# A recorded attention and two-network kernel: the list scheduler takes other transfer rates, and the weight sums of the second network leave from one contiguous corner

## The chip, the cores and the metric

The kernel runs on one core of a Trainium2 chip. The metric is the device time of one execution in microseconds (us), the median of several runs. TensorE (PE) multiplies matrices, VectorE (DVE), ScalarE (ACT) and GpSimd (POOL) work on elements, and SyncE (SP) issues the DMA transfers, which 16 DMA engines of the core carry out. SBUF is the on-chip memory with 128 partitions; PSUM holds the eight banks that matmuls write.

## The reference

Windowed attention with 32 global tokens, then two feed-forward networks over all 2304 tokens, all in float32.

```python
# q_l, k_l, v_l: (4, 8, 512, 64); q_g, k_g, v_g: (4, 8, 32, 64)
s_g = scale * q_g @ [k_g, k_l].T
out_g = softmax(s_g) @ [v_g, v_l]
s_ll = where(abs(pos_q - pos_k) <= 32, scale * q_l @ k_l.T, -1e9)
s_l = concatenate([scale * q_l @ k_g.T, s_ll])
out_l = softmax(s_l) @ [v_g, v_l]
x = concatenate([out_g, out_l]) as (2304, 512)
# first network: 512 -> 1536 -> 512
g = x @ w_gate
x = (g * sigmoid(g) * (x @ w_val)) @ w_out
# second network: 512 -> 2048 -> 512
h = x @ w_in
out = (maximum(h, 0) + alpha * minimum(h, 0)) @ w_out2
```

The weights of both networks come to the chip as float64 words.

## The kernel before, in words

**The work.** Every product is made in three passes over operands that are split into a high and a low part (type fp32r), so that float32 accuracy is kept. The first network is done in visits: `visit1(b, fs, ...)` takes the 512 tokens of batch b through one half of the hidden columns, f by f: `mm12` makes the gate bank `g` and the value bank `v` from the inputs `xa` (12 matmuls each), ACT makes `sg` (silu), DVE the product `t`, ACT the high half of `h` and DVE its low half, and `down(f)` adds 12 matmuls into the four banks `acc0` to `acc3`. A third visit (line 1239 on) and the whole second network use seven products of half-size blocks in place of eight, for which sums of weight blocks are wanted beside the weights.

**Preparing weights.** A piece of float64 weights is loaded into a buffer `dbl` (`dbl_tile`, two buffers, dbl_111 and dbl_112), turned into float32 in a buffer `raw` (raw_131, raw_132) by `convert_steps` (L753): two ACT instructions (raw<-dbl, then dbl<-dbl in place) and three on DVE. For the second network the generator `w2_prepare` (L861) does that for 16 pieces. `out_to` (L868) splits each piece into its high and low half in the `dbl` buffer and stores it to DRAM (`w2s`; the names in the profile are w2sx and w2so, 1 MB each). For each of the eight pieces of the input weights it also makes the sums of blocks (`block_sums`, L850) in a second raw buffer. Those sums (key "s", w2ss in the profile) leave another way while the recording is on: the high half is written by ACT into a free part of `xa`, namely the last 128 of the 640 columns in each of its eight rows, and stored from there, 8 pieces of 512 bytes for each partition; the low half is made in place and stored from raw. `pumper` (L1079) calls the generator: at each pump a counter grows by `P["w2n"]`, and the generator goes one step for each whole number reached. What is left of the generator when the recording ends goes on in the straight part. The sums of the first network's weights (`w1_sums`, L823) are made by DVE in the two buffers of `ex` (y_139 and y_166 or y_167 in the listings) and stored as w1ss4v, w1ss5g and so on; the split weights of the first network are stored as w1s and loaded again later (w<-w1s4g).

**The order.** The first part of the kernel (attention, and the first network for batches 0 to 2, about 421 us) isn't issued as it is written. `Planner` (L58) records each instruction with its reads and writes; `price` (L124) gives it a duration, `graph` (L154) finds what depends on what, and `order` (L180) simulates the four engines and picks, at each step, the ready instruction with the earliest due time. Transfers are simulated as one channel that moves `DMA` KB a microsecond; `flush` (L265) then issues everything in that order on each engine. All these instructions have line L272 in the profile. The buffers were given out when the work was recorded, so the order decides when each comes free. What follows `flush` (the third visit, the second network) is written straight. The lines of `order` on a transfer:

```python
if e == "sync":
    y += 0.45
    dma = max(dma, y + 1.0) + atoms[i][0].lat
    done[i] = [dma + 0.9]
```

Of the kernel before, what the change touches and what calls it, by code (L numbers as in the profile page):

```python
# [10 lines left out]
F32 = mybir.dt.float32  # L11
F32R = mybir.dt.float32r
# [4 lines left out]
ACTF = mybir.ActivationFunctionType  # L17
ALU = mybir.AluOpType

B, H, S, G, D = 4, 8, 512, 32, 64  # L20
# [4 lines left out]
N3 = 320  # L25
NAMES = ("b11", "t2", "t3", "t1", "b21", "t4", "b22")
NT = 384
# [10 lines left out]
    lo0=0.0, lo1=0.0, lo2=0.0, lo3=0.0, hi0=0.0, hi1=0.25, hi2=0.25, hi3=0.5,  # L38
    wl0=2, wl1=2, wd=2, tsim=False,
    hq0=0.0, hq1=0.0, hq2=0.0, hq3=0.0, pr_s=0, pr_pv=0, pr_conv=0, pr_hilo=0, pr_st=0, pr_ld=0, pr_h=0,  # L40
    pr_xp=0, pr_acc=0, pr_lda=0, wage=3, w2n=1.7, w2max=200, cp0=0.5, cp1=0.0,
)


# [13 lines left out]
class Planner:  # L58
# [6 lines left out]


    ENGINES = ("tensor", "vector", "scalar", "sync")
    TABLE, DMA, START, LAST = 1.28, 405.0, 0.75, 10.0

    def __init__(self, tc):  # L70
        self.tc, self.nc = tc, tc.nc
# [108 lines left out]
    def order(self):  # L180
        atoms, preds = self.atoms, self.graph()
        N = len(atoms)
        size = [sum(o.cost for o in a) for a in atoms]
        eng = [a[0].eng for a in atoms]
        before = [sorted({j for e in p.values() for j, _ in e}) for p in preds]
        for i, b in enumerate(before):
            assert not b or b[-1] < i
        after = [[] for _ in atoms]
        for i, b in enumerate(before):
            for j in b:  # L190
                after[j].append(i)
        at, target = 0.0, [0.0] * N
        for i in range(N):
            target[i] = at
            if eng[i] == "tensor":
                at += size[i]
        due = [0.0] * N
        for i in reversed(range(N)):
            d = target[i] if eng[i] == "tensor" else min(target[i] + self.SLACK, at - self.LAST)
            for j in after[i]:  # L200
                d = min(d, due[j] - size[i] - atoms[i][-1].lat)
            due[i] = d
        free = {e: self.START for e in self.ENGINES}
        table, dma = None, 0.0
        left = [len(b) for b in before]
        done = [None] * N
        ready = {e: {} for e in self.ENGINES}

        def data(i):
            t, off = 0.0, 0.0  # L210
            for m, o in enumerate(atoms[i]):
                for j, k in preds[i].get(m, ()):
                    x = done[j][k] - off
                    if eng[j] == eng[i]:
                        x -= atoms[j][k].lat if eng[i] != "sync" else 0.0
                    elif eng[i] == "tensor":
                        x += self.MARGIN
                    t = max(t, x)
                off += o.cost
            return t  # L220

        for i in range(N):
            if not left[i]:
                ready[eng[i]][i] = 0.0
        plan = []
        while len(plan) < N:
            best = None
            for e in self.ENGINES:
                if ready[e]:
                    t = max(free[e], min(ready[e].values()))  # L230
                    if best is None or t < best[0]:
                        best = (t, e)
            t, e = best
            cand = [i for i, r in ready[e].items() if r <= t + self.LOOK]

            def rank(i):
                f = atoms[i][0].table
                return due[i] + (self.SWITCH if f and f != table else 0.0)

            i = min(cand, key=rank)  # L240
            x = max(t, ready[e].pop(i))
            f = atoms[i][0].table
            if f and f != table:
                x += self.TABLE
                table = f
            done[i] = []
            y = x
            if e == "sync":
                y += 0.45
                dma = max(dma, y + 1.0) + atoms[i][0].lat  # L250
                done[i] = [dma + 0.9]
            else:
                for o in atoms[i]:
                    y += o.cost
                    done[i].append(y + o.lat)
            free[e] = y
            plan.append(i)
            for j in after[i]:
                left[j] -= 1
                if not left[j]:  # L260
                    ready[eng[j]][j] = data(j)
        self.end = max(free.values())
        return plan
# [22 lines left out]
class Slots:  # L286
# [11 lines left out]
    def next(self, tag):  # L298
        return self.turn.get(tag, 0) % self.sizes[tag][0]
# [22 lines left out]
def kernel(  # L322
# [11 lines left out]
    nc = Planner(tc)  # L334
# [14 lines left out]
    const = ctx.enter_context(tc.tile_pool(name="const", bufs=1))  # L349
# [17 lines left out]

    ident = const.tile([128, 128], F32, name="ident")
    ex = Slots(const, {"y30": (1, 1024), "y31": (1, 1024)})
    xa = const.tile([128, 2, 4, 640], F32R, name="xa")  # L370
    yp = [const.tile([128, 2, 4, 256], F32, name=f"yp{b}") for b in range(B - 1)]
    y3 = {}

# [308 lines left out]
    def dbl_tile():  # L682
        i = ring["d"] = (ring["d"] + 1) % ND
        if i == 2 and st["k"] < mark[2] - 4:
            return yp[2].rearrange("p h m c -> p (h m c)").bitcast(I64)
        return dblp.tile([128, 1024], I64, tag="dbl", name="dbl")
# [154 lines left out]
    w2s = {}  # L841
# [19 lines left out]
    def w2_prepare():  # L861

        def land(n):
            dbl = dbl_tile()
            nc.sync.dma_start(out=dbl, in_=w2[n // 2, n % 2])
            return dbl

        def out_to(key, raw):  # L868
            w2s[key] = dram.tile([128, 2, 1024], F32, name="w2s%s%d" % key)
            if key[0] != "s" or not nc.recording:  # L870
                t = dbl.bitcast(F32R).rearrange("p (h c) -> p h c", h=2)
                yield from split(t, raw)
                nc.sync.dma_start(out=w2s[key], in_=t.bitcast(F32))
                return
            hi, lo = xa.rearrange("p h k c -> p (h k) c")[:, :, S:640], raw.rearrange("p (k c) -> p k c", c=128)
            st["tail"] = True
            nc.scalar.activation(out=hi, in_=lo, func=ACTF.Copy)
            yield
            nc.vector.tensor_tensor(out=lo.bitcast(F32R), in0=lo, in1=hi, op=ALU.subtract)
            nc.sync.dma_start(out=w2s[key][:, 0].rearrange("p (k c) -> p k c", c=128), in_=hi.bitcast(F32))  # L880
            nc.sync.dma_start(out=w2s[key][:, 1], in_=raw)
            st["tail"] = False

        dbl = land(0)
        for n in range(2 * NJ):
            ahead = land(n + 1) if n + 1 < 2 * NJ else None
            yield
            raw = raw_tile()
            yield from convert_steps(dbl, raw)
            yield  # L890
            if n % 2 == 0:
                s = raw_tile()
                yield from block_sums(s, raw)
            yield from out_to(("xo"[n % 2], n // 2), raw)
            if n % 2 == 0:
                for _ in range(1 if nc.recording else 6):
                    yield
                yield from out_to(("s", n // 2), s)
            dbl = ahead
# [136 lines left out]
    if True:  # L1036
# [92 lines left out]
        p = pumper(P["ns1"], mark[2] + LAG, P["wr0"], P["g1"])  # L1129
        visit1(0, GA, False, p, after_f=reload(GB, GA))  # L1130
        visit1(0, GB, True, p, boundary=lambda: xprep(1))
        p = pumper(P["ns2"], mark[3] + LAG, P["wr2"], P["g2"])
        visit1(1, GB, False, p, after_f=summing(reload(GA, GB)))
        visit1(1, GA, True, p, after_f=summing(lambda f, ps: None), boundary=lambda: xprep(2))
        p = pumper(P["ns3"], mark[4] + 9, P["wr3"], P["g3"])
        visit1(2, GA, False, p, after_f=reload(GB, GA))

        ops1, w3, place, sums = {}, {}, {}, {}
# [20 lines left out]
        def oper(flat, n):  # L1159
            return flat[:, 0:4 * n].rearrange("p (h k c) -> p h k c", h=2, k=2)  # L1160
# [21 lines left out]
        def third():  # L1182

            while wq:
                wload(True)
            while st.get("tail"):
                next(w2gen)
            flat = xa.rearrange("p h k c -> p (h k c)")
            for i, name in enumerate(("t3", "t1", "b21", "t4")):
                ops1[name] = oper(flat[:, 4 * N3 * i:4 * N3 * i + 4 * N3], N3)  # L1190
            x_split(2, ops1["b11"], (0, 0))
            for name in ("t2", "t3", "t1"):
                x_split(2, ops1[name], sums[name])
            x_split(2, ops1["b21"], (1, 0))
            x_split(2, ops1["t4"], sums["t4"])

        visit1(2, GB, True, p, after_f=before_third, boundary=third)
        while wq:
            wload(True)
# [19 lines left out]
        ops = {}  # L1219
# [109 lines left out]
        for j in range(NF1 // 2):  # L1329
# [10 lines left out]
            h = hring[j % 2]  # L1340
# [37 lines left out]
        x_split(0, ops["t1"], t1)  # L1378
        t4 = next(sums)[1]
        x_split(0, ops["t3"], next(sums)[1])  # L1380
        flat = xa.rearrange("p h k c -> p (h k c)")
        for i, name in enumerate(("b21", "t4", "b22")):
            ops[name] = oper(flat[:, 4 * NT * i:4 * NT * i + 4 * NT], NT)
        x_split(0, ops["b21"], (1, 0))
        x_split(0, ops["t4"], t4)
        x_split(0, ops["b22"], (1, 1))
# [194 lines left out]
```

## Time and profile before

| | before |
|---|---|
| median of 3 runs | 897.06 us (897.03 to 897.11) |
| the profiled execution | 896.01 us |
| its span in the profile | 894.2 us |
| TensorE busy | 866.7 us (97%) |
| DVE busy | 692.1 us (77%) |
| ACT busy | 528.2 us (59%) |
| DMA queue 1 | 238.19 MB, 70.8% of the 16 engines' span |

The span is what the profiler saw of the instructions; the profiled execution's own time is 1.8 us longer. A row of an engine's timeline gives the start in us, the busy time, the engine, the line, the operation with the tile that it writes and the one that it reads, the size, how many follow one another, and in brackets the idle time before it with what ended that. On SP a row is the issue of a transfer; when it landed is in the view of DMA issues. A row of stretches gives the stretch, its length, the busy time of PE, PEld (weight loads), DVE, ACT and POOL with their instructions, the granted clock as a share of full speed, the share of time that the DMA engines were busy, and GB/s.

### The profile page before, as it was taken

How to read it: one execution, taken by the hardware profiler on the slowest of the kernel's cores; microseconds unless marked ns; L12 is line 12 of the kernel's file. 1: busy time of each engine (PE TensorE's matmuls, PEld its weight loads, DVE VectorE, ACT ScalarE, POOL GpSimd, SP SyncE). 2: the span in 40 equal slices, each digit the busy share in tenths (PEclk: the TensorE clock that was granted, in tenths of full speed). 3: DMA queues.
4: the chain of work that ended last, by engine and by line, in shares of the span. 5: the costliest groups of instructions: out<-in, count | busy, mean ns of one | idle time of the engine just before them, and what ended most of it. 6: DMA issues, size and time to landing. Idle time of an engine off the chain costs nothing.

```text
span 894.2 us, 17315 instructions
## 1 busy us (share of the span) xinstructions
PE 866.7 (97%) x6868; PEld 749.0 (84%) x6868; DVE 692.1 (77%) x1442; ACT 528.2 (59%) x1051; POOL 0.7 (0%) x6
## 2 busy tenths in 40 slices
PE   6799999999899999899999999999999999999997
PEld 5577778787688787778999999999999999989996
DVE  4997889969778865688666677777896777977776
ACT  5889999767667688554333346434555434554442
POOL 0000000000000000000000000000000000000000
PEclk9999999999999999999999999999999999999999
DMA  9899899798986789985656665546375554675731
GB/s 360 300 393 414 334 354 361 289 351 321 407 358 219 301 323 370 335 306 192 212 189 206 237 247 212 228 156 267 142 266 229 211 213 172 252 272 225 280 141 60
DMA packets 48833, 239.30 MB, mean 268 GB/s; under 512 B 4848, under 2 KB 13680, under 8 KB 26480
## 3 DMA queue, kind: packets, MB, share of 16 engines
q1 hardware_dynamic: 48752, 238.19, 70.8%
q8 instruction: 54, 0.88, 0.4%
q14 instruction: 27, 0.22, 0.1%
HBM read 183.38 MB, written 54.79 MB: 266 GB/s over the span
## 4 chain that ended last, share of the span: by engine, by line
PE 78%; DMA 10%; ACT 5%; DVE 5%; issue 1%; SPq 0%; ACTq 0%; DVEq 0%
PE ps_acc L1451 21%; PE ps_g L1239 9%; PE ps_v L1239 9%; PE ps_a L1239 8%; PE acc L272 8%; PE v L272 7%; PE g L272 7%; PE a L272 5%; PE ps_acc L1296 3%; DMA dbl<-in_w_dram 3%; DMA w2so<-dbl 2%; PE ps_a L1296 2%; DMA w2sx<-dbl 2%; DVE dbl L272 1%; DMA yp<-in_w_dram 1%
## 5 line engine op out<-in xcount | busy, mean ns | idle before, releaser
L1451 PE MATMUL ps_acc<-w,hring 128*128 128x512 f32 x816 | 194.2, 391 | 0.0
L1451 PEld LDWEIGHTS ps_acc<-w,hring 128*128 128x128 f32 x816 | 152.0, 188 | 30.1 <-ACT hring L1420 0.3
L272 PE MATMUL acc<-h,w 128*128 128x512 f32 x432 | 108.2, 399 | 3.1 <-ACT h L272 2.2
L272 PE MATMUL g<-xa,w 128*128 128x512 f32 x432 | 107.8, 398 | 2.5 <-ACT sg L272 1.6
L272 PE MATMUL v<-xa,w 128*128 128x512 f32 x432 | 107.1, 396 | 0.2 <-issue 0.2
L1415 ACT ACTIVATE r<-c 128x384 f32<-128x384 f32 (+1 forms) x96 | 47.8, 498 | 92.9 <-DVE c L1247 92.9
L272 PEld LDWEIGHTS acc<-h,w 128*128 128x128 f32 x432 | 81.0, 191 | 22.3 <-ACT h L272 2.5
L1456 DVE TENSOR_TENSOR oacc<-ps_acc,oacc 128x512 f32<-128x512 f32 x119 | 81.9, 691 | 22.2 <-PE ps_acc L1451 20.9
L272 PEld LDWEIGHTS g<-xa,w 128*128 128x128 f32 x432 | 78.9, 188 | 22.8 <-ACT sg L272 3.0
L272 PEld LDWEIGHTS v<-xa,w 128*128 128x128 f32 x432 | 79.3, 188 | 18.6 <-issue 1.8
L1420 ACT ACTIVATE hring<-g 128x384 fp32r<-128x384 f32 (+1 forms) x96 | 48.6, 506 | 55.9 <-DVE g L1417 55.6
L272 ACT ACTIVATE e<-e,mx 128x128 f32<-128x128 f32 (+1 forms) x136 | 57.2, 423 | 14.6 <-DVE mx L272 14.2
L1421 DVE TENSOR_TENSOR hring<-g,hring 128x384 fp32r<-128x384 f32 (+1 forms) x96 | 51.1, 532 | 18.9 <-ACT hring L1420 16.1
L1417 DVE SCALAR_TENSOR_TENSOR g<-g,nal,r 128x384 f32<-128x384 f32 (+1 forms) x96 | 56.8, 591 | 10.4 <-ACT g L1416 9.7
L272 ACT ACT_TABLE_LOAD x46 | 59.0, 1283 | 8.0 <-PE g L272 6.6
L1416 ACT ACTIVATE g<-c 128x384 f32<-128x384 f32 (+1 forms) x96 | 47.9, 499 | 13.9 <-DVE hring L1421 13.9
L1239 PE MATMUL ps_g<-xa,w 128*128 128x320 f32 (+1 forms) x288 | 53.3, 318 | 0.2
L1239 PE MATMUL ps_v<-xa,w 128*128 128x320 f32 (+1 forms) x288 | 53.2, 319 | 0.1
L1239 PE MATMUL ps_a<-w 128*128 128x384 f32 (+1 forms) x288 | 51.4, 326 | 0.0
L1239 PEld LDWEIGHTS ps_g<-xa,w 128*128 128x128 f32 x288 | 47.1, 188 | 1.9 <-ACT p L1255 0.4
L1239 PEld LDWEIGHTS ps_v<-xa,w 128*128 128x128 f32 x288 | 46.8, 188 | 1.6 <-DVE u L1263 0.4
L1239 PEld LDWEIGHTS ps_a<-w 128*128 128x128 f32 x288 | 47.9, 188 | 0.1
(211 smaller groups left out, 1397.7 us busy)
## 6 DMA issues: line engine op xcount, KB each, us to landing
dbl<-in_w_dram SPq DMA_DIRECT2D x28, 1024.0 KB, 8.0
w<-w2so SPq DMA_DIRECT2D x24, 1024.0 KB, 5.3
w<-w2sx SPq DMA_DIRECT2D x24, 1024.0 KB, 4.8
w<-w2ss SPq DMA_DIRECT2D x24, 1024.0 KB, 6.4
v<-in_v_dram SPq DMA_DIRECT2D x15, 1024.0 KB, 10.0
qk<-in_qk_dram SPq DMA_DIRECT2D x14, 688.0 KB, 9.5
w2sx<-dbl SPq DMA_DIRECT2D x8, 1024.0 KB, 8.0
w2so<-dbl SPq DMA_DIRECT2D x8, 1024.0 KB, 9.7
```

The lines of the kernel that those rows point to most:

```text
L272: last[o.eng] = getattr(getattr(self.nc, o.eng), o.op)(*o.args, **o.kw)
L1239: nc.tensor.matmul(out=o[:, 0:n], lhsT=left(name, a, k), rhs=x[name][:, b, k, 0:n], start=(i == 0), stop=(i == 5),)
L1296: mm = nc.tensor.matmul(out=o, lhsT=a, rhs=x, start=(first and e == 0 and not second), stop=((j, f, e) == (NF1 // 2 - 1, 0, 2) and i not i ...
L1415: nc.scalar.activation(out=rr, in_=u, func=ACTF.Relu)
L1416: nc.scalar.activation(out=g, in_=u, func=ACTF.Relu, scale=-1.0)
L1417: nc.vector.scalar_tensor_tensor(out=g, in0=g, scalar=nal[:, i:i + 1], in1=rr, op0=ALU.mult, op1=ALU.add)
L1420: nc.scalar.activation(out=hi, in_=g, func=ACTF.Copy)
L1421: nc.vector.tensor_tensor(out=lo, in0=g, in1=hi, op=ALU.subtract)
L1451: nc.tensor.matmul(out=o, lhsT=a, rhs=x, start=(i == 0), stop=(i == 5))
L1456: nc.vector.tensor_tensor(out=oacc[tb], in0=o, in1=oacc[tb], op=ALU.add)
```

## The change

It has three parts. In `order`, the channel of the simulation moves 385 KB/us, not 405; a transfer may start 0.3 us after its issue begins, not 1.45, and is seen by others 1.9 us after its end, not 0.9. `w2n` is 2, not 1.7. And `xa` is allotted as one flat tile: its first 4096 columns are the eight rows of 512 columns, and the 1024 columns behind them are `tail`, into which the high half of the sums is written, and from which it is stored, 4 KB in one piece for each partition.

```diff
-    ... w2n=1.7, ...
+    ... w2n=2, ...
...
-    TABLE, DMA, START, LAST = 1.28, 405.0, 0.75, 10.0
+    TABLE, DMA, START, LAST = 1.28, 385.0, 0.75, 10.0
...
             if e == "sync":
+                dma = max(dma, y + 0.3) + atoms[i][0].lat
+                done[i] = [dma + 1.9]
                 y += 0.45
-                dma = max(dma, y + 1.0) + atoms[i][0].lat
-                done[i] = [dma + 0.9]
...
-    xa = const.tile([128, 2, 4, 640], F32R, name="xa")
+    xall = const.tile([128, 16 * N3], F32R, name="xa")
+    xa = xall[:, 0:8 * S].rearrange("p (h k c) -> p h k c", h=2, k=4)
+    tail = xall[:, 8 * S:8 * S + 1024]
...
-            hi, lo = xa.rearrange("p h k c -> p (h k) c")[:, :, S:640], raw.rearrange("p (k c) -> p k c", c=128)
             st["tail"] = True
-            nc.scalar.activation(out=hi, in_=lo, func=ACTF.Copy)
+            nc.scalar.activation(out=tail, in_=raw, func=ACTF.Copy)
             yield
-            nc.vector.tensor_tensor(out=lo.bitcast(F32R), in0=lo, in1=hi, op=ALU.subtract)
-            nc.sync.dma_start(out=w2s[key][:, 0].rearrange("p (k c) -> p k c", c=128), in_=hi.bitcast(F32))
+            nc.vector.tensor_tensor(out=raw.bitcast(F32R), in0=raw, in1=tail, op=ALU.subtract)
+            nc.sync.dma_start(out=w2s[key][:, 0], in_=tail.bitcast(F32))
             nc.sync.dma_start(out=w2s[key][:, 1], in_=raw)
```

In the two places where all of `xa` is used as one flat area (`third` and the end of the third visit), `xall` takes the place of the rearranged tile.

What these numbers do to the order is seen in the listings of the instructions of each engine, here at three places. The first is SP where the first network's sums w1ss4v are stored. Before:

```order
L272 DMA w2sx_165<-dbl_111 128x2048
L272 DMA w2ss_167<-raw_132 128x1024
L272 DMA w_134<-w1s1g 128x2048
L272 DMA dbl_111<-in_w_dram 128x1024
L272 DMA w1ss4v<-y_166 128x1024
L272 DMA w2so_170<-dbl_112 128x2048
L272 DMA w1ss4g<-y_139 128x1024
L272 DMA w_135<-w1s2g 128x2048
```

With the change, where that store stands now:

```order
L272 DMA dbl_112<-in_w_dram 128x2x512
L272 DMA w1s8o<-w_144 128x2048
L272 DMA w1s10g<-w_137 128x2048
L272 DMA w1ss4v<-y_167 128x1024
L272 DMA v_110<-in_v_dram 128x2048
L272 DMA v_108<-in_v_dram 128x2048
L272 DMA w1s11g<-w_138 128x2048
L272 DMA dbl_112<-in_w_dram 128x1024
```

The store has gone from SP's row 76 to its row 62, ahead of the loads of the next attention pairs' v.

The second place is ACT in the second visit to batch 1, behind the pt (the transposed probabilities) of an attention pair; dbl_111 holds a piece of the second network's weights there. Before:

```order
L272 ACTIVATE h_151<-t_150 128x512
L272 ACTIVATE dbl_112<-raw_132 128x1024
L272 ACTIVATE raw_131<-dbl_111 128x1024
L272 ACTIVATE dbl_111<-dbl_111 128x1024
L272 ACT_TABLE_LOAD
L272 ACTIVATE sg_148<-g_103 128x512
L272 ACTIVATE yp_95<-a_114 128x2x256
L272 ACTIVATE dbl_111<-raw_131 128x1024
L272 ACTIVATE h_152<-t_150 128x512
```

With the change:

```order
L272 ACTIVATE h_151<-t_150 128x512
L272 ACTIVATE dbl_112<-raw_132 128x1024
L272 ACT_TABLE_LOAD
L272 ACTIVATE sg_148<-g_103 128x512
L272 ACTIVATE yp_95<-a_114 128x2x256
L272 ACTIVATE raw_131<-dbl_111 128x1024
L272 ACTIVATE dbl_111<-dbl_111 128x1024
L272 ACTIVATE h_152<-t_150 128x512
L272 ACTIVATE dbl_111<-raw_131 128x1024
```

The two conversions of the piece in dbl_111 have gone behind the table load, sg and yp, and the split dbl_111<-raw_131 behind h_152.

The third place is SP where the piece of that conversion is loaded. Before:

```order
L272 DMA w_136<-w1s3g 128x2048
L272 DMA w2sx_173<-dbl_111 128x2048
L272 DMA w2ss_174<-xa 128x8x128
L272 DMA dbl_111<-in_w_dram 128x1024
L272 DMA w2ss_174<-raw_131 128x1024
L272 DMA w_137<-w1s4g 128x2048
L272 DMA w1ss5g<-y_139 128x1024
L272 DMA w1ss0v<-y_166 128x1024
L272 DMA w_144<-w1s2o 128x2048
```

With the change:

```order
L272 DMA w_136<-w1s3g 128x2048
L272 DMA w2ss_172<-xa 128x1024
L272 DMA w2sx_171<-dbl_111 128x2048
L272 DMA w2ss_172<-raw_131 128x1024
L272 DMA w_137<-w1s4g 128x2048
L272 DMA w1ss5g<-y_139 128x1024
L272 DMA dbl_111<-in_w_dram 128x1024
L272 DMA w_144<-w1s2o 128x2048
```

The load of dbl_111 has gone behind the store of raw_131, the load of w_137 and the store w1ss5g; the store from the corner is 128x1024 in place of 128x8x128, and stands ahead of w2sx.

## Rows read from the trace of the kernel before

**Rows 1.** The page, busy time of each engine, share of the span, instructions.

```profile
PE 866.7 (97%) x6868; PEld 749.0 (84%) x6868; DVE 692.1 (77%) x1442; ACT 528.2 (59%) x1051; POOL 0.7 (0%) x6
```

**Rows 2.** Busy time of each engine in three stretches, granted clock (PEclk), DMA share.

```profile
60.00:200.00 140.00, 139.32 (x1589) 110.18 (x1591) 119.59 (x271) 126.82 (x246) 0.00 (x0) 1.00 0.92 352
234.00:238.00 4.00, 4.00 (x19) 2.83 (x17) 3.55 (x7) 2.02 (x4) 0.00 (x0) 0.65 1.00 387
440.00:894.00 454.00, 449.72 (x2484) 415.58 (x2482) 345.60 (x655) 197.88 (x423) 0.00 (x0) 1.00 0.56 211
```

**Rows 3.** TensorE's timeline, the groups with idle time before them, and one for comparison.

```profile
206.79 1.16 PE L272 MATMUL a<-qk 64*32 64x128 f32 x64 [0.68 <-DVE o L272]
...
220.85 0.66 PE L272 MATMUL a<-ident,o 128*128 128x128 f32 x4 [0.44 <-ACT pt L272]
...
225.12 2.88 PE L272 MATMUL acc<-h,w 128*128 128x512 f32 x12
228.66 1.11 PE L272 MATMUL a<-qk 64*32 64x256 f32 x24 [0.67 <-ACT yp L272]
231.97 0.50 PE L272 MATMUL acc<-h,w 128*128 128x512 f32 x1 [2.19 <-ACT h L272]
233.37 4.37 PE L272 MATMUL acc<-h,w 128*128 128x512 f32 x11 [0.91 <-DVE h L272]
...
370.70 0.66 PE L272 MATMUL a<-ident,o 128*128 128x128 f32 x4 [2.49 <-ACT pt L272]
```

**Rows 4.** DVE's timeline at the store of w1ss4v.

```profile
197.59 0.69 DVE L272 TENSOR_TENSOR y<-w 128x512 f32<-128x512 f32 x1 [8.27 <-DMA w1ss4v<-y]
```

**Rows 5.** ACT's timeline from 224 to 232 us.

```profile
224.06 1.13 ACT L272 ACTIVATE raw<-dbl 128x1024 f32<-128x1024 f32 x1 [1.31 <-DMA w2ss<-raw]
...
227.53 0.60 ACT L272 ACTIVATE sg<-g 128x512 f32<-128x512 f32 x1
...
231.28 0.63 ACT L272 ACTIVATE h<-t 128x512 fp32r<-128x512 f32 x1 [0.74 <-DVE t L272]
```

**Rows 6.** SP's timeline, issues at 216 to 219 us.

```profile
216.34 0.33 SPq L272 DMA_DIRECT2D dbl<-in_w_dram  x1
...
218.59 0.32 SPq L272 DMA_DIRECT2D w1ss5g<-y  x1
```

**Rows 7.** DMA issues at 216.3 and 234.7 us, KB, us from issue to landing.

```profile
dbl<-in_w_dram SPq DMA_DIRECT2D x1, 1024.0 KB, 5.9
...
dbl<-in_w_dram SPq DMA_DIRECT2D x1, 1024.0 KB, 14.1
```

**Rows 8.** Chain of waits from 300 to 400 us: start, us, what.

```profile
350.23 10.75 DMA w2so<-dbl
361.00 7.96 DMA dbl<-in_w_dram
369.04 1.12 ACT raw L272
```

**Rows 9.** SP's timeline at 279 us.

```profile
279.16 0.32 SPq L272 DMA_DIRECT2D w2sx<-dbl  x1
279.53 0.43 SPq L272 DMA_DIRECT2D w2ss<-xa  x1
```

**Rows 10.** DMA issues at 279 us, KB, us from issue to landing.

```profile
w2sx<-dbl SPq DMA_DIRECT2D x1, 1024.0 KB, 4.0
w2ss<-xa SPq DMA_DIRECT2D x1, 512.0 KB, 6.2
```

**Rows 11.** Two short stretches, the last column is GB/s.

```profile
283.16:285.73 2.57, 2.57 (x29) 2.06 (x18) 2.50 (x7) 2.18 (x4) 0.00 (x0) 1.00 1.05 238
255.96:258.54 2.58, 2.58 (x14) 2.10 (x13) 2.55 (x4) 1.94 (x11) 0.00 (x0) 1.00 0.99 411
```

**Rows 12.** ACT's timeline at 109 us.

```profile
108.75 0.60 ACT L272 ACTIVATE sg<-g 128x512 f32<-128x512 f32 x1
109.25 1.15 ACT L272 ACTIVATE raw<-dbl 128x1024 f32<-128x1024 f32 x1
```

More of the change, by code (lines that the diff above doesn't have):

```diff
@@ L40 @@
     hq0=0.0, hq1=0.0, hq2=0.0, hq3=0.0, pr_s=0, pr_pv=0, pr_conv=0, pr_hilo=0, pr_st=0, pr_ld=0, pr_h=0,
-    pr_xp=0, pr_acc=0, pr_lda=0, wage=3, w2n=1.7, w2max=200, cp0=0.5, cp1=0.0,
+    pr_xp=0, pr_acc=0, pr_lda=0, wage=3, w2n=2, w2max=200, cp0=0.5, cp1=0.0,
 )
@@ L1187, in third @@
                 next(w2gen)
-            flat = xa.rearrange("p h k c -> p (h k c)")
             for i, name in enumerate(("t3", "t1", "b21", "t4")):
-                ops1[name] = oper(flat[:, 4 * N3 * i:4 * N3 * i + 4 * N3], N3)
+                ops1[name] = oper(xall[:, 4 * N3 * i:4 * N3 * i + 4 * N3], N3)
             x_split(2, ops1["b11"], (0, 0))
@@ L1380 @@
         x_split(0, ops["t3"], next(sums)[1])
-        flat = xa.rearrange("p h k c -> p (h k c)")
         for i, name in enumerate(("b21", "t4", "b22")):
-            ops[name] = oper(flat[:, 4 * NT * i:4 * NT * i + 4 * NT], NT)
+            ops[name] = oper(xall[:, 4 * NT * i:4 * NT * i + 4 * NT], NT)
         x_split(0, ops["b21"], (1, 0))
```

## Prediction

> **What bounds the kernel now.** I read the busy shares first, then each engine in stretches, then TensorE's own queue for its idle times, then who ended each of them. TensorE is busy 866.7 of 894.2 us [rows 1]. The stretches tell where the other 27.5 us lie: from 60 to 200 us it is idle for 0.68 us, and from 440 to 894 us it is busy 449.72 of 454 us [rows 2]. So the change can gain only where TensorE waits between 200 and 440 us (the first 60 us, with some 14 us, are mostly the start and stay). TensorE's idle rows [rows 3] give the stock: 0.68 us at 206.79, 0.44 at 220.85, 0.67 at 228.66, 2.19 at 231.97, 0.91 at 233.37 and 2.49 at 370.70, in all 7.38 us. The four stops around 230 us cost more than their sum: the eleven matmuls from 233.37 us took 4.37 us, while twelve of the same kind at 225.12 took 2.88, so eleven should take 2.64, and 1.73 us are lost to the clock, which was granted at 0.65 from 234 to 238 us [rows 2, 3]. That is full speed (2.4 GHz) given up for the lower level (1.2 GHz) in part of that stretch, after 3.77 us of idle time within 6 us. The releasers of all these stops are DVE and ACT, and these wait for transfers: that is what the planner's constants place.
>
> The sum is made against the profiled execution, 896.01 us, 1.05 us below the median of 897.06; its result is moved up by 1.05 at the end. 0.2% of this time is 1.8 us, about what a measurement can tell from no change.
>
> **The change, part by part.**
>
> *Nothing is added.* ACT, SP and TensorE issue as many instructions as before and DVE one fewer; the loads and stores carry the same bytes; ACT loads its tables 46 times in both. One store of prepared second-network weights (w2so, 1 MB) moves from the straight part into the recording, because the generator is advanced 2 steps a pump, not 1.7. I take 0 for it: its work on DVE and ACT is hidden by TensorE's matmuls, since after 440 us those engines are busy 346 and 198 of 454 us [rows 2]; without that cover it would be one 1 MB transfer, 5.9 us by the nearest load [rows 7]. The larger matter is the order.
>
> *DVE at 189 us.* DVE stands for 8.27 us until the store of weight sums w1ss4v has left its buffer y, at 197.59 us [rows 4]. After that it catches up without a pause until its o at 206 us, for which TensorE waits 0.68 us; the pt at 220.85 (0.44 us) follows from the same lateness [rows 3]. In the changed order this store stands 14 rows earlier on SP, ahead of the stores and loads that now delay it, and the other buffer is used. DVE does not get all of 8.27 us, since its inputs come from TensorE; about half of it is six times the larger stop. **-1.1 us** (bounds: 0, if another operand is as late; -1.12).
>
> *ACT at 224 to 232 us.* ACT now waits 1.31 us for a store (w2ss from raw) and then makes two conversions of a loaded weight half before the table load and sg [rows 5]; TensorE's qk product waits for the yp behind sg (0.67 us), then acc for h (2.19) and for h's low half on DVE (0.91) [rows 3]. In the changed order the table load, sg and yp come before the conversions, and h stands one conversion earlier. ACT's chain then begins with the end of the previous conversion (222.7 us: the wait of 1.31 us ends at 224.06): table load and sg end at 224.6, yp at 225.2, two conversions of 1.13 at 227.4 and h at 228.0, its low half 0.69 later, 228.7, or 1.5 us earlier if DVE and ACT arrive earlier by the step above. TensorE needs it near 228.5, after the acc of 225.12, the qk product with its 24, and 8 more that now come ahead of acc. So all four parts go: 0.67 + 2.19 + 0.91 + 1.73 = 5.50 us. I take **-5.0 us**, a tenth being left for an h that is late by a few tenths. The bounds are -5.50 and 0.
>
> This hangs on the load of the weight half (dbl). Before, it is issued at 216.34 us and lands 5.9 us later [rows 6, 7]. In the changed order it stands behind the store w1ss5g, issued at 218.59 us now [rows 6]: if nothing else came earlier, it would be issued at about 219.0. SP must wait there for DVE's sums; everything on SP behind that store waits with it: this load, and then the weight w from w1s2o, which is behind that store in both orders. With 5.9 us it lands at 224.9, in time for a conversion that begins at 225.2. The same load, issued at 234.7 us in the full queue, took 14.1 [rows 7].
>
> *ACT at 370 us.* TensorE waits 2.49 us for pt, behind ACT's conversion raw, which waits for the load dbl [rows 3]. The chain of waits shows why: a store of 10.75 us (w2so) must leave dbl, then the load takes 7.96 us, and only then raw runs at 369.04 [rows 8]. The order on ACT there is as before. What can shorten it is the transfers. A w2ss store from the corner of xa, in 512 byte rows, was issued at 279.53 us and took 6.2 us; the store before it in the queue, issued at 279.16, took 4.0 [rows 9, 10]. So the one landed at 285.73, 2.57 us after the other at 283.16, and in that stretch the chip moved 238 GB/s; in a stretch of contiguous stores 40 us earlier it moved 411 [rows 11], at which 524 KB take 1.28 us. A contiguous store may save up to 2.57 - 1.28 = 1.3 us of queue time; one of the eight such stores lies in the 20 us before this wait, and one more some 35 us earlier. I take 1.8 of 2.49: one and a half stores' savings, **-1.8 us** (bounds: 0, if the store was slowed by others in the queue and not by its rows; -2.49, the whole wait).
>
> The Trainium skill speaks against this step. Its page "DMA: Bandwidth & Descriptors", section Specifications, gives 512 bytes as the least transfer that goes at line rate, with a read-modify-write only below that; by it these rows already ran at full speed, and without the 1.8 us the time would be 891.4. The trace here disagrees so far, with 238 against 411 GB/s, though other transfers share that queue.
>
> *ACT at 109 us: a new wait.* The sg at 108.75 us, half a microsecond ahead of a conversion of 1.15 us now [rows 12], stands in the changed order behind that conversion and the one after it, 1.15 + 1.13 us less the overlap, so sg ends about 2.2 us later, at 111.6. Its bank g is needed by the next matmuls at 111.2: **+0.4 us** (bounds: 0, where ACT got there earlier; +2.2).
>
> *The other moves* (the start, and 60 to 165 us, where ACT is busy nearly throughout) I take at 0: their cover is that TensorE is idle only 0.68 us in 140 [rows 2]. Below it: a conversion that goes ahead of exponentials at the start may give or take 1.0 us.
>
> **Sum:** -1.1 - 5.0 - 1.8 + 0.4 = -7.5 us, 888.5 us profiled, **889.6 us** for the median.
>
> **The rivals.**
>
> 1. *The store's shape saves nothing*: the corner store was slow by its place in the queue, not by its rows. The gains at 189 and 224 us stay, the one at 370 does not: -1.1 - 5.0 + 0.4 = -5.7, **891.4 us**. For it: other transfers lie in the same 2.57 us. Against it: 238 GB/s there, though 1 MB had just left at 4.0 us. The page of the Trainium skill named above stands on this side.
>
> 2. *Gained at 230, given back at 370.* TensorE comes 6.1 us earlier to a place where the chain of transfers from 300 to 370 us decides [rows 8]; stores and loads of dbl follow one another there through the one buffer and the queue, whatever TensorE does. Then pt comes as late as before less what the transfers save, at most 2.5 us: 897.06 - 2.5 = **894.6 us**. For it: the 18.7 us before raw are one store and one load [rows 8]. Against: ACT and DVE in that chain come earlier with TensorE.
>
> 3. *Slower: the load behind the store of sums.* If the dbl load, now behind w1ss5g on SP, takes more than some 10.75 us, h is as late as before and the gain of 5.0 is gone; that is the deciding point. At the 14.1 us of [rows 7] it lands at 233.1, two conversions, h and its low half end at 236.7, some 3.3 us after 233.37, and with the clock down for longer about +4: **901 us**. For it: 14.1 us was seen 16 us later. Against: at this place now it is 5.9.
>
> 4. *The moves cancel.* Almost every row of the recording is moved a little; new waits of 1 to 2 us at places that I took at 0 eat the gain: **897 us**.
>
> **How the numbers follow.** The forecast has a chance of 0.52, rival 1 0.11, rival 2 0.13, rival 3 0.14, rival 4 0.10. Faster by over 0.2% are the forecast and rivals 1 and 2: 0.76; within 0.2% rival 4: 0.10; slower rival 3: 0.14. The range: all that can go, -1.12 - 5.50 - 2.49 and -1.0 at the start, is -10.1, hence 886.9, and I allow 0.9 below for stops too small to list: 886.0. Above it takes in rivals 1 and 2 and the near half of rival 4: 896.5. That leaves out rival 3 and part of rival 4, some 0.2.
>
> **What would show it.** In the profile of the changed kernel DVE has no wait of several us at 189; TensorE runs from 225 to 240 us without a stop of over 0.5 us and with the clock granted at 1.00; the dbl load near 218 us lands within 8 us; the corner store of 0.5 MB lands about 1.3 us behind its neighbour; the wait at 370 is below 1 us; a wait of some tenths stands at 111. Wrong would be: a wait of 2 us or more for pt, h or sg between 240 and 400 us where now there is none (rival 2), ACT's conversion at 225 waiting for dbl (rival 3), or TensorE idle for more than 2 us between 60 and 200 us (rival 4).

## The result, and the profile after

The changed kernel takes 885.44 us (median of 4 runs, 883.09 to 887.76), the kernel before 897.04 on the same chip: ratio 0.9872, 95% interval 0.9843 to 0.990. The forecast was 889.6 us with a range from 886.0. The direction was right, the gain of 11.6 us is half as much again as the 7.5 of the forecast, and the time lies 0.56 us below the range. The profiled execution took 886.36 us (span 884.6), 9.65 us less than that of before. One run of the experiment margin07 below took 1671.88 us and is left out of that experiment's figures.

The page, and two stretches of the changed kernel (the same columns as in [rows 1] and [rows 2]):

```profile
PE 864.1 (98%) x6868; PEld 749.6 (85%) x6868; DVE 690.8 (78%) x1441; ACT 527.2 (60%) x1051; POOL 0.7 (0%) x6
```

```profile
60.00:200.00 140.00, 139.97 (x1610) 111.36 (x1609) 126.20 (x283) 129.16 (x242) 0.00 (x0) 1.00 0.95 364
200.00:240.00 40.00, 40.00 (x373) 32.08 (x372) 35.42 (x79) 31.69 (x54) 0.00 (x0) 1.00 0.99 394
```

The stretch from 200 to 240 us was this in the kernel before, with 4.96 us without a matmul and a granted clock of 0.96:

```profile
200.00:240.00 40.00, 35.04 (x304) 26.45 (x293) 36.94 (x80) 30.20 (x48) 0.00 (x0) 0.96 0.95 361
```

It is filled now, and all of it at full speed. TensorE's timeline, to be held against [rows 3]:

```profile
222.54 2.88 PE L272 MATMUL acc<-h,w 128*128 128x512 f32 x12
225.35 1.54 PE L272 MATMUL a<-qk 64*32 64x256 f32 x32
226.82 3.01 PE L272 MATMUL acc<-h,w 128*128 128x512 f32 x12
...
359.94 0.66 PE L272 MATMUL a<-ident,o 128*128 128x128 f32 x4 [0.40 <-ACT pt L272]
386.00 3.02 PE L272 MATMUL g<-xa,w 128*128 128x512 f32 x12 [0.91 <-ACT sg L272]
```

The qk product is one group of 32, and acc follows without a stop; 2.49 us at 370 have become 0.40; the stop for sg behind it has grown from 0.37 to 0.91. ACT and SP, against [rows 5] and [rows 6, 7]:

```profile
220.13 0.60 ACT L272 ACTIVATE sg<-g 128x512 f32<-128x512 f32 x1
220.62 0.59 ACT L272 ACTIVATE yp<-a 128x512 f32<-128x512 f32 x1
221.69 1.14 ACT L272 ACTIVATE raw<-dbl 128x1024 f32<-128x1024 f32 x1 [0.48 <-DMA dbl<-in_w_dram]
...
224.41 0.63 ACT L272 ACTIVATE h<-t 128x512 fp32r<-128x512 f32 x1 [0.55 <-DVE t L272]
```

sg and yp come ahead of the conversions, which wait for the load of dbl now, 0.48 us. That load was issued at 214.90 and landed 6.8 us later: rival 3 did not come about.

DVE's order at this place changed as well, which no listing ahead of the prediction shows. Two rows of the kernel before, then two of the changed kernel:

```profile
230.23 0.42 DVE L272 TENSOR_TENSOR raw<-raw 128x256 f32<-128x256 f32 x1
230.57 0.68 DVE L272 TENSOR_TENSOR t<-v,sg 128x512 f32<-128x512 f32 x1
...
223.69 0.68 DVE L272 TENSOR_TENSOR t<-v,sg 128x512 f32<-128x512 f32 x1
224.29 0.68 DVE L272 TENSOR_SCALAR raw<-raw 128x1024 f32<-128x1024 f32 x1
```

Before, t came behind DVE's steps on the converted piece (raw); now it comes ahead of them. Counted from the start of the same acc group (225.12 us before, 222.54 now), sg ends 1.8 us ahead of it in place of 3.0 behind [rows 5], and t begins 1.2 us behind it in place of 5.5. DVE's wait of 8.27 us [rows 4] is gone too: its longest from 173 to 212 us is 1.41 us.

Where the 9.65 us came from is seen when the same matmul is looked up in both timelines and its starts are subtracted. The differences of the changed kernel's two profiles to that of before, by stretch (times of the kernel before; after_again is the second profile, below):

| from, to | forecast | after | after_again |
|---|---|---|---|
| 0 to 50 us (the start) | 0 | +0.58 | -1.20 |
| 50 to 102 | 0 | -1.10 | -1.09 |
| 102 to 173 | +0.4 | -0.24 | +0.32 |
| 173 to 228 (DVE's wait) | -1.1 | -1.82 | -1.83 |
| 228 to 264 (yp, h, the clock) | -5.0 | -6.12 | -6.14 |
| 264 to 371 (dbl, pt) | -1.8 | -2.07 | -2.66 |
| 371 to 436 | 0 | +1.13 | +0.35 |
| sum | -7.5 | -9.64 | -12.25 |

After 436 us nothing changes. The start differs from execution to execution of any kernel here; the rest is the change, but for some tenths by which its two profiles differ.

### The profile page after: what moved, and what is told of

Same layout as the page of the kernel before. It is cut to its first block, busy times and chain, and to the rows that moved or that the text cites. A ratio compares the mean times of both kernels' runs of the same rounds, so it can differ in the third digit from the quotient of the medians.

```text
span 884.6 us, 17317 instructions
## 1 busy us (share of the span) xinstructions
PE 864.1 (98%) x6868; PEld 749.6 (85%) x6868; DVE 690.8 (78%) x1441; ACT 527.2 (60%) x1051; POOL 0.7 (0%) x6
## 4 chain that ended last, share of the span: by engine, by line
PE 88%; DMA 6%; DVE 2%; ACT 2%; issue 1%; SPq 0%; ACTq 0%; DVEq 0%
PE ps_acc L1450 21%; PE acc L272 10%; PE g L272 10%; PE v L272 10%; PE ps_g L1239 9%; PE ps_v L1239 9%; PE ps_a L1239 8%; PE a L272 7%; PE ps_acc L1296 3%; DMA w2so<-dbl 2%; PE ps_a L1296 2%; DMA dbl<-in_w_dram 2%; DMA qk<-in_qk_dram 1%; DMA yp<-in_w_dram 1%; DMA hring<-w1ss1v 1%
## 5 line engine op out<-in xcount | busy, mean ns | idle before, releaser
L272 PE MATMUL acc<-h,w 128*128 128x512 f32 x432 | 106.1, 394 | 0.0
```

The costliest lines, as they stand in the source:

```text
L272: last[o.eng] = getattr(getattr(self.nc, o.eng), o.op)(*o.args, **o.kw)
```

## The experiments

Each ratio is to runs of the kernel before on the same chip; 23 to 35 such runs stand beside each group. It is an estimate from all runs of both kernels, and differs from the ratio of the two medians by up to 0.002.

**The change once more.** No edit.

> The changed kernel once more, unaltered. If the gain is that of the order alone, every profile of it shows TensorE without a stop between 200 and 240 us, and the time is 885.4 us within the 2.5 us that the first four runs spread. If a part of the gain was luck of one profile, a stop of some tenths to 2 us stands between 60 and 360 us in this one. The spread itself: if it comes from the start (the first qk load ended 1.8 us later in the first profile than in that of the kernel before), the late part shows before 10 us again or is gone, and the time moves with it.

884.35 us, ratio 0.988 (0.9856 to 0.9903), no stop of over 0.2 us from 60 to 360 us. The first qk product started at 6.13 us, not 7.77 as in the first profile. The gain is the order's, and it repeats within 0.1 us in the stretches from 173 to 264 us.

**The store's shape.** In corner_rows the changed kernel stores from rows of 512 bytes:

```diff
-    xall = const.tile([128, 16 * N3], F32R, name="xa")
-    xa = xall[:, 0:8 * S].rearrange("p (h k c) -> p h k c", h=2, k=4)
+    xa = const.tile([128, 2, 4, 640], F32R, name="xa")
...
-            nc.sync.dma_start(out=w2s[key][:, 0], in_=tail.bitcast(F32))
+            nc.sync.dma_start(out=w2s[key][:, 0].rearrange("p (k c) -> p k c", c=128), in_=hi.bitcast(F32))
```

> The changed kernel with the sums' high half in the old corner of xa, 512 byte rows; the planner's numbers and w2n as in the change, so the order of the recording is the same up to two rows at its end. Theory of the prediction (a store in 512 byte rows takes some 1.3 us more of the queue): the stop before pt near 360 us, 0.40 us in the changed kernel, is back at about 2.2 us, and the time is some 1.8 us above the changed kernel, 887.3. Rival (rows of 512 bytes go at line rate): the same stop, and the time within 0.5 us of the changed kernel.

887.64 us, ratio 0.9914 (0.9892 to 0.9935), 3.3 us above after_again on the same chip. The stop for pt is back:

```profile
362.02 0.66 PE L272 MATMUL a<-ident,o 128*128 128x128 f32 x4 [1.84 <-ACT pt L272]
```

From 264 to 371 us it gains only 0.63 us where the change gains 2.07 and 2.66, so in these profiles the shape is worth 1.4 to 2.0 us there; the rest of the 3.3 lies within what executions differ by. The same two stores, at 206 and 334 us, in the changed kernel and then in corner_rows:

```profile
w2ss<-xa SPq DMA_DIRECT2D x1, 512.0 KB, 4.5
...
w2ss<-xa SPq DMA_DIRECT2D x1, 512.0 KB, 6.8
```

```profile
w2ss<-xa SPq DMA_DIRECT2D x1, 512.0 KB, 5.4
...
w2ss<-xa SPq DMA_DIRECT2D x1, 512.0 KB, 7.7
```

These two take 0.9 us longer in rows, but they are two of eight. Over all eight the store in rows is between 1.5 us shorter and 1.0 longer, 0.2 longer in the mean, since other transfers share the queue. The rate is read better where the row packets are nearly alone: 1020 of the 1062 packets in the first stretch, of corner_rows. The second is the same place in the changed kernel (columns as in [rows 2]):

```profile
273.70:275.60 1.90, 1.90 (x55) 1.51 (x54) 0.69 (x1) 1.89 (x3) 0.00 (x0) 1.00 1.04 305
...
272.00:275.50 3.50, 3.50 (x63) 2.81 (x62) 1.39 (x2) 3.47 (x5) 0.00 (x0) 1.00 1.03 414
```

At the next such store it is 365 against 405 GB/s. At these rates 524 KB in rows take 0.1 to 0.5 us longer, which is an estimate. How 1.4 to 2.0 us at one stop come of that is not shown. The Trainium skill's rule ("DMA: Bandwidth & Descriptors", Specifications) that 512 bytes go at line rate doesn't hold for this store: 305 and 365 GB/s with rows are less than the 414 and 405 without them.

tail_only is the reverse: the kernel before with the flat tile and nothing else.

> The kernel before with the contiguous corner alone; the planner's numbers and w2n as before, and with them the order as before but for a few rows at the end. Theory of the prediction: the stops around 230 us stay (0.67, 2.19, 0.91), the one at 370 us falls from 2.49 to about 0.7, and the time is 895.2 us. Rival (line rate): 897.0 within 0.5 us, the stop at 370 as before.

894.84 us against 893.93, ratio 1.000 (0.9982 to 1.0019): no gain that can be told. The stop at 370 fell to 1.48 us, but TensorE's start and its stop at 206 us (1.57) were later in this profile, and a TensorE that comes later waits less there. Inconclusive by itself: the forecast, a ratio of 0.998, lies at the interval's lower edge.

**ACT's order without DVE's t.** Five instructions of the kernel before are moved in the plan: ACT's two conversions and its split, and DVE's two steps that take up the conversions (the expectation says seven; numbers are those of the recording):

```diff
-        for i in self.order():
+        for i in moved(self.order()):
...
+MOVES = [([692, 693, 694, 710], 668), ([733], 689)]
```

`moved` takes each list out of the plan and puts it behind the instruction named with it.

> The kernel before with seven instructions moved and nothing else: at 224 us ACT's two conversions of dbl_111 go behind the table load, sg and yp, the split of raw_131 behind h_152, and DVE's two steps on the converted piece behind o and rc. Planner, corner and w2n as before. Theory: this one place is the 5.5 us of the prediction, so the stops 0.67, 2.19 and 0.91 and the low clock at 234 us are gone, those at 206 and 220 us stay, and the time is 892 us (5 below). Rival 2 (given back at 370): the stop at 370 us grows by as much as is gained, and the time is 895 to 897 us.

897.88 us, ratio 1.0027 (1.0008 to 1.0045): slower, against both expectations. The stop for yp went, but those for h grew from 2.19 and 0.91:

```profile
233.72 0.50 PE L272 MATMUL acc<-h,w 128*128 128x512 f32 x1 [3.27 <-ACT h L272]
236.53 5.06 PE L272 MATMUL acc<-h,w 128*128 128x512 f32 x11 [2.31 <-DVE h L272]
```

DVE's timeline shows why:

```profile
229.92 1.23 DVE L272 SCALAR_TENSOR_TENSOR raw<-raw,dbl 128x1024 int32<-128x1024 int32 x1
231.19 0.42 DVE L272 TENSOR_TENSOR raw<-raw 128x256 f32<-128x256 f32 x1
231.65 0.42 DVE L272 TENSOR_TENSOR raw<-raw,raw 128x256 f32<-128x256 f32 x1
231.99 0.42 DVE L272 TENSOR_TENSOR raw<-raw 128x256 f32<-128x256 f32 x1
232.32 0.68 DVE L272 TENSOR_TENSOR t<-v,sg 128x512 f32<-128x512 f32 x1
...
235.79 0.68 DVE L272 TENSOR_TENSOR h<-t,h 128x512 fp32r<-128x512 f32 x1
```

t, from which h is made, stands behind the block sums of the converted piece, as in the kernel before. With the conversion later, so is t, and h with it.

**DVE's order too.** both_swap adds t and the low half of h, dve_swap moves these and ACT's h alone:

```diff
-MOVES = [([692, 693, 694, 710], 668), ([733], 689)]
+MOVES = [([688], 719), ([692, 693, 694, 710, 689, 691], 668)]  # both_swap
+MOVES = [([688], 719), ([689], 668), ([691], 711)]  # dve_swap
```

> The kernel before with ACT's order at 224 us as in the run act_swap, and in addition DVE's t ahead of its three steps on the converted piece and h's low half ahead of the last of them, as the changed kernel has it. New theory: DVE's order, not ACT's, was what made h late, since t stood behind the block sums of a piece that had just been converted. By the rows of act_swap (sg ends at 226.1 us, yp at 226.6, conversions at 228.6, DVE free at 226.3) t ends at 227.0, h at 229.2 and its low half at 229.9, about when TensorE is through with the qk product; so the stops of 0.67, 2.19 and 0.91 us and the low clock go, some 5 us: the ratio to the kernel before is 0.994. Rival 2 (given back at 370 us): ratio 0.998 to 1.000, with a stop at 370 of 4 us or more.

> The kernel before with DVE's t and h's low half moved ahead of the block sums, and ACT's h ahead of the split; ACT's conversions stay ahead of the table load and sg. New theory: most of the gain is here. sg ends near 228.1 us as before, t near 228.8, h at 229.5, its low half near 230.7; the stop for yp (0.67 us) stays, those for h shrink from 3.1 to under 1 us and the low clock goes: some 4 us, ratio 0.9955. Theory of the prediction (ACT's order holds it): the stops for h stay over 2 us, ratio 0.998 or more.

both_swap 892.91 us, 0.9974 (0.9955 to 0.9992); dve_swap 892.39, 0.9971 (0.9957 to 0.9986). In both_swap t comes at 226.99 and h without a stop. Between 228 and 237 us the start of the same matmuls moves from 1.61 us behind the kernel before to 4.18 ahead: 5.8 us gained at the place where 5.0 were forecast. Then part is lost, most of it at a new stop:

```profile
239.25 0.66 PE L272 MATMUL a<-ident,e 128*128 128x128 f32 x4 [1.72 <-DVE mx L272]
```

and at 264 us 3.4 of the 5.8 us are left. The stop at 370 went too, without any change of the stores. dve_swap keeps yp's stop (0.83) and has 0.45 for h, and gains 4.1 us at the place: as its expectation had it there, though its ratio was to be 0.9955. DVE's two rows with ACT's h are thus worth most of the gain, and ACT's conversions the rest.

**DVE's wait at 189 us alone.** early_store makes the last block sums of w1ss4v at 160 us and stores them there:

```diff
+MOVES = [([621, 622], 620), ([623], 557)]
```

> The kernel before with three instructions moved: the last two block sums of w1ss4v are made at 160 us with the first two, and its store goes out behind w1ss3g, some 25 us earlier. ACT's order, the planner, the corner and w2n as before. DVE's wait of 8.27 us at 189 us goes in every theory. Theory of the prediction (this place is worth the stops at 206 and 220 us alone): 1.1 us, ratio 0.9988, and the stops for h at 232 us stay over 2 us. New theory (DVE is the engine that is late at 230 us, and its 8.27 us is the cause): DVE comes to 210 us some 4 us earlier, its split, the store w2sx and the load behind it go out earlier by as much, and the stops for yp and h shrink to under 1 us in all, with the clock at 1.00: some 6 us, ratio 0.9935.

894.15 us, 0.9992 (0.9973 to 1.0012). The stops at 206 and 220 us are gone, and from 173 to 228 us it gains 1.83 us, as much as the changed kernel. Those for h stay: 2.20 and 0.77 us, with the eleven matmuls at 5.06. ACT's conversion waits 1.88 us for its store instead of 1.31: an earlier DVE doesn't bring h earlier while the orders stand. The prediction's step was right, and the theory in its place falls.

**Both places by hand**, early_both, and early_both_tail with the flat tile on top:

> The moves of early_store and of both_swap together, 10 instructions; planner, corner and w2n as before. If the changed kernel's gain up to 240 us is these two places, no stop is left from 200 to 245 us (that at 239 for DVE's mx in both_swap too), 6.6 us and more are gained there, and the ratio is 0.9925, or 0.990 with the 2.5 us at 370 us, which had gone in both_swap. Rival (given back at 370): ratio 0.997, as both_swap.

> The hand moves of early_both and the contiguous corner on the old planner's order. early_both was 0.996, with new stops for DVE's mx and o (1.75, 1.24 us) behind the moved place and none at 370 us. If the corner saves some 1.3 us of queue time a store wherever it stands, but no stop near a store is left to shorten, the ratio is 0.996 as early_both within 0.002. If the corner is what keeps the gain from being given back, the stops behind 235 us shrink and the ratio is 0.990 or less.

890.97 us, 0.9959 (0.9939 to 0.9979), and 889.64, 0.9949 (0.9931 to 0.9968). At 237.67 us early_both is 7.65 us ahead; of that 0.68 stood at 102, so 7.0 come from the two places. Then DVE is late again:

```profile
235.81 0.66 PE L272 MATMUL a<-ident,e 128*128 128x128 f32 x4 [1.75 <-DVE mx L272]
239.47 0.33 PE L272 MATMUL a<-ident,o 128*128 128x128 f32 x1 [0.25 <-ACT pt L272]
259.89 0.66 PE L272 MATMUL a<-ident,o 128*128 128x128 f32 x4 [0.49 <-ACT pt L272]
265.80 1.16 PE L272 MATMUL a<-qk 64*32 64x128 f32 x64 [1.24 <-DVE o L272]
```

These four, 3.73 us, are what the changed kernel doesn't have: its planner ordered what follows as well. With the flat tile the last two shrink (0.39 us left) and no stop stands at 370 in either; the two ratios overlap.

**The planner's numbers one by one.** The changed kernel with a single number altered:

```diff
-    TABLE, DMA, START, LAST = 1.28, 385.0, 0.75, 10.0
+    TABLE, DMA, START, LAST = 1.28, 405.0, 0.75, 10.0  # rate405; d375, d380, d395 alike
...
-                dma = max(dma, y + 0.3) + atoms[i][0].lat  # oldsync, with y += 0.45 ahead
-                done[i] = [dma + 1.9]
+                dma = max(dma, y + 1.0) + atoms[i][0].lat
+                done[i] = [dma + 0.9]
...
-    w2n=2, MARGIN=0.5
+    w2n=1.7 (w17), MARGIN=0.7 (margin07)
```

> The changed kernel with the planner's rate put back to 405 KB/us; issue and landing times, w2n and the contiguous corner as in the change. If the slower rate is what puts the work into a good order (transfers that come later than planned stop an engine), the stops of 0.5 to 2 us come back somewhere between 100 and 400 us and the ratio is 0.992 or more. Rival (the landing times do it, or w2n): 0.988 as the changed kernel.

> The changed kernel with the planner's old times for the start and the landing of a transfer; the rate 385, w2n = 2 and the contiguous corner stay. Its order differs from the changed kernel's in a few rows of SP, ACT and DVE alone. If the order is what counts, and not how true the model is, the ratio is 0.988 within 0.002. Rival (the landing times do it): 0.992 or more, with stops for transfers.

> The changed kernel with w2n back at 1.7: generator steps are spread over more pumps. Rate, landing times and contiguous corner as in the change. If the rate of 385 is what puts the order right, the ratio stays at 0.988 to 0.990. Rival (the order is a matter of chance, and any of the three numbers turns it): stops of 0.5 to 2 us somewhere between 100 and 400 us, ratio 0.993 or more.

> The changed kernel with the planner's rate at 375 KB/us, 3% below the change's. Theory (a rate at or below what the queue moves gives a good order): ratio 0.988 to 0.990, stops under 0.5 us from 60 to 360 us. Rival (385 is a lucky number of an order that jumps): ratio 0.993 or more.

> The changed kernel with the planner's rate at 380 KB/us, 1.3% below. If a true rate makes a good order, 380 is as true as 385, and the ratio is 0.987 to 0.990. If the order jumps with any number, it lies between d375 (0.996) and the change (0.988) without a rule, with at least one stop of over 0.8 us between 60 and 400 us.

> The changed kernel with the planner's rate at 395 KB/us, halfway to rate405 (1.001). If too fast a rate brings the stops back by degrees, the ratio is 0.993 to 0.996. If the order jumps, it is near one of the two ends: 0.988 or 1.001.

> The changed kernel with the planner's margin for TensorE's inputs at 0.7 us, not 0.5: a number that has nothing to do with transfers, but moves many rows. If the measured transfer numbers carry the gain, it stays: 0.987 to 0.990. If chance has a large part, the ratio is 0.992 or more, with stops of 0.5 to 2 us where the changed kernel has none.

| run | us | ratio (95%) | longest stops, 52 to 360 us |
|---|---|---|---|
| rate405 | 894.95 | 1.0007 (0.9994 to 1.002) | 2.07 at 233, 0.90 at 234 |
| d395 | 893.52 | 0.9998 (0.9981 to 1.0016) | 4.60 at 231 |
| the change, again | 884.35 | 0.988 (0.9856 to 0.9903) | none over 0.2 |
| d380 | 890.63 | 0.9966 (0.9944 to 0.9989) | 1.66 at 53, 0.92 at 103 |
| d375 | 891.61 | 0.9963 (0.9944 to 0.9982) | 2.66 at 100, 0.86 at 234 |
| oldsync | 886.36 | 0.991 (0.989 to 0.9931) | 0.90 at 227 |
| w17 | 888.52 | 0.9931 (0.9906 to 0.9956) | 0.83 at 226 |
| margin07 | 887.58 | 0.9943 (0.9919 to 0.9966) | 1.34 at 100, 1.37 at 232 |

The two kinds of loss look like this, in d395 and in d375:

```profile
231.24 0.80 PE L272 MATMUL acc<-h,w 128*128 128x512 f32 x1 [4.60 <-ACT h L272]
232.31 4.56 PE L272 MATMUL acc<-h,w 128*128 128x512 f32 x11 [0.28 <-DVE h L272]
```

```profile
100.31 5.87 PE L272 MATMUL acc<-h,w 128*128 128x512 f32 x12 [2.66 <-ACT h L272]
```

Both times a stop for h of over 2 us is followed by acc matmuls that take 1.7 to 2.0 times their time; the granted clock was 0.57 from 231 to 237 us in d395 and 0.50 from 100 to 106 in d375. With the old rate the old stops stand at the old places (2.07 us for h at 233, and DVE's wait for w1ss4v, 8.30 us), whatever else is changed: in this combination there is no gain without the new rate. No run has the new rate alone on the kernel before. The old landing times with the new rate cost little (0.991, between its two expectations), and their order differs from the changed kernel's in a few rows. But w2n at 1.7 gives back 0.005 of the 0.012 gained, 1.3% less than 385 most of it, and a margin that has nothing to do with transfers half. In w17, d375, d380, d395 and margin07 the expectation that came true is the one by which the order jumps. Whether 380 or 385 is nearer to the truth no run tells, and yet 380 is worse: 385 is one good order among orders that jump. That a truer simulation makes better orders is not shown; the one sign of it is that 375 to 385 are all better than 395 and 405.

## Why the prediction was right or wrong

The places were right, and so was most of the mechanism. The time fell below the range because gains were taken too small (the moves taken at 0 from 50 to 102 us, DVE's wait, and the slower matmuls behind the stops for h) and because 1.05 us were added for the median.

- **What bounds it, and the places**: right. All the listed stops between 200 and 240 us are gone, and the one at 370 nearly.
- **-1.1 at DVE's wait**: right in cause (early_store removes the stops at 206 and 220, and not those for h), small in size: 1.8 us from 173 to 228. The idle times were read as the cost. The matmuls behind the two stops began 0.75 and 0.62 us earlier where 0.68 and 0.44 us of idle time went, and a wait for sg at 217 us that shows as 0.08 us idle gave 0.4.
- **-5.0 at 224 to 232**: the place and nearly the size are right, 6.1 us in both profiles. The step that failed is the chain "table load and sg end at 224.6, ... h at 228.0": it let t follow sg and v at once, and gave the gain to ACT's order. (In the changed kernel too t begins 3.0 us after sg has ended, which costs TensorE nothing there.) In the order before, t stands on DVE behind the piece's block sums; with ACT's rows moved and t left there, the kernel is slower (act_swap). The changed order moves t as well, which the prediction's listings, of ACT and SP, did not show. The bound of 5.50 was too small for another reason: the clock's loss was priced on eleven matmuls alone. The one ahead of them took 0.50 us, and the qk product, cut in two, 1.75 where it now takes 1.54 in one piece.
- **The dbl load**: right. 5.9 us was assumed, 6.8 measured, and h came in time.
- **-1.8 at 370**: the size is near, 2.1 and 2.7 us, but the price behind it was too high, so this is luck in part. The two stores that it was read from landed 2.57 us apart, and 1.44 and 1.14 us apart in the two profiles of the changed kernel; in corner_rows, with the rows put back, 1.72. So the shape has 0.3 to 0.6 of the 1.3 us. The 238 GB/s held half a microsecond, from 285.0 to 285.5 us, in which the DMA engines were busy 0.28; and the stretch of 411 GB/s, 27 us earlier and not 40, held packets of a load beside the stores. corner_rows still loses 1.4 to 2.0 us at this stop, and in both_swap the stop went with the stores left in rows: what else shortened it stays open.
- **+0.4 at 109 and the rest at 0**: the wait is there, 0.28 us: sg ends at 110.91, and the g behind it begins 1.06 us after the transposes began, not 0.78. The step that failed is **the other moves at 0**: the stretch from 50 to 102 us lost its stop of 0.49 us for yg at 79 and smaller ones, 1.1 us in all, in corner_rows and oldsync too. 0.68 us of idle time was read as cover, where it was a small stock of its own.
- **Nothing counted behind 371**: 0.4 to 1.1 us were given back there. In both profiles the sg at 386 us comes later, behind a conversion that waits for its load; in the first, TensorE also waits 0.46 us for ACT at 424 us.
- **Rival 2, given back**: it is real for the hand moves (1.72 us at 239, 3.73 in early_both), but at DVE's next rows, not at 370. Rival 1 holds for most of the store's price, not for the stop. Rivals 3 and 4 did not come about.
- **From the profiled time to the median**: 1.05 us was added, since three runs of the kernel before agreed within 0.08 us. On the other chips its runs lie between 888.96 and 899.27 us, with medians of 893.93 to 894.91. So three runs did not show a spread that is 8 us or more elsewhere; whether that first chip is slower or its few runs were high is not shown. The difference of medians is 11.6 here and 9.6 beside after_again. The changed kernel's profiled execution was itself 0.92 us above its median, so the step of +1.05 went the wrong way. A range from 886.0 was too narrow at that end.

The median was forecast about 4.1 us too high. Of that, 2.14 us lie between the two profiles: 1.7 too little gain from 50 to 173 us, 0.7 at DVE's wait, 1.1 at h and the clock and 0.3 at 370, against 0.6 that the start lost and 1.1 lost behind 371. The other 2.0 us are the 1.05 that was added and the 0.92 of the profiled execution.

## What to carry to other kernels

When a scheduler moves a chain, list its rows on every engine that the chain crosses: a chain from ACT over DVE to ACT and back is late at its worst row, and a move on one engine alone can make it later. Price a stop on TensorE with the slower matmuls behind it, the first of them included. A simulated rate that gives a good order is not therefore a true one: try its neighbours before reading anything from it.

## What the runs showed of the hardware that was not expected

While a store of 512 KB left in rows of 512 bytes, the DMA engines moved 305 and 365 GB/s; with the same bytes in pieces of 4 KB, and larger packets of other transfers beside them, 414 and 405 (corner_rows, the changed kernel); from issue to landing the eight stores differ by -1.5 to +1.0 us. The start is the least steady part of this kernel: the first qk product began between 5.59 and 7.77 us after the span's start in the profiles of this case, and at 7.77 and 6.13 in the two of the changed kernel itself, and matmuls at 50 us stood from 1.2 us ahead of the kernel before's to 1.7 behind. A stop of 2.66 us for h at 100 us was followed by twelve matmuls in 5.87 us, with a granted clock of 0.50 (the lower level, 1.2 GHz); without such a stop they take 2.88.
